# A wkv attention and expert-layer kernel on one core: VectorE's look at the chunk sums of w moves ahead of the output sum

## The chip, the core and the metric

The kernel runs on one NeuronCore of one Trainium2 chip. The metric is the device time of one execution in microseconds (us); a median of several runs is compared. TensorE is called PE in the profile, its weight loads PEld, VectorE DVE, ScalarE ACT, GpSimd POOL and SyncE SP.

## The reference, cut to what matters

```
for t in range(S):                                  # B=4, H=8, S=768, D=48
    y[:, :, t] = r_t @ (state + (u * k_t) v_t)      # per batch and head
    state = w_t[:, None] * state + k_t v_t
x = y as 3072 rows of 384
expert = argmax(x @ w_gate); gate = softmax(x @ w_gate)[expert]
out = gate * (relu(x @ w1[expert]) @ w2[expert])    # 8 experts, 384 -> 1024 -> 384
```

The first half is a linear attention with a decay w per position and channel; the second sends each of the 3072 rows to one of eight experts.

## The kernel before

**Tiling.** A half sequence of 384 positions is cut into 6 chunks of 64. Two heads share the 128 partitions (64 each, called sides), so a pass over one pair of heads and one half sequence is one iteration `i`, and there are NI = 32 of them: 4 batches, 4 pairs, 2 halves. Two iterations, an even one and the odd one after it, make a unit `un`. The attention fills the first half of the span, the experts the second. The order in which each engine gets its instructions is the order of the program text: nothing is reordered, and each engine works its own list through in that order, stopping at an instruction until the semaphores it needs are there.

**One iteration.** Iteration `i` prepares iteration `i + 2` and finishes `i - 2`. Its front, in the order of the text: ScalarE copies the chunk products of `i - 1` out of PSUM (`kv_out`, L605, out `PT`); TensorE transposes w of `i + 2` into bank `pw` (`tr_w`, L472) and the scaled keys of `i` into bank `pk` (`kb`, L550), ScalarE copies them out (`kb_out`, L557). VectorE adds the output of `i - 3` (`y_out`, L652: `py` plus `qv`, out `xr`), does a piece of routing if one is queued (`more`), and in even iterations scans the states of the last unit (`states`, L610: `PT` and `AT` in, `TT` out). Then it computes the decay of `i + 2`: a scan to `L` (L511), three small operations (L516, L517) and a scan to `F` (L524), both scans from bank `pw`. Behind that stands, in every fourth iteration, the look at w.

The body follows: GpSimd multiplies `qv` (L640) and `XB` (L537); TensorE transposes r (L480) and computes the scores (`sc`, L569); ScalarE copies the states to `RA` (L618) and `RB` (L621, even iterations; on VectorE, L623, for the last two units) and one side's scores to `XB` (L579); VectorE masks the other side's scores into `XA` (`sc_out`, L577). TensorE transposes k (L480), multiplies u (L488); ScalarE copies `kT` (L502) and `qs` (L494), and spreads w of `i + 3` into `gw` (`spread_w`, L446). VectorE multiplies `XA` (L535), `Kd` (L528) and `rk` (L441). TensorE ends its list for the iteration with the chunk sums of w (`w_sum(i + 2)`, L452), the chunk products (`kv(i)`, L597) and the output of `i - 2` (`y_mm`, L632), which reads `RA`, `RB`, `XA` and `XB`.

**The look at w.** `w_sum` writes 32 partitions of columns 144 to 271 of bank `pb` (`psP[1]`), a quarter for each of four iterations. `w_flag(g)` (L456) lets VectorE read all 128 x 128 of them once the four are there and puts the largest value of each partition into a column of `flags`; the flags decide at the end whether the slow path is needed. It runs in iterations 2, 6, 10, ..., 30, eight times. The same bank `pb` holds, in columns 0 to 143, half of what `kv` writes and `kv_out` reads. The four sums that `w_flag` in iteration 4g+2 reads were all issued by the end of iteration 4g+1, ahead of that iteration's `kv` and `y_mm`; the next sum, which overwrites a quarter, is issued near the end of iteration 4g+2.

```
def w_flag(g):
    nc.vector.tensor_scalar(wchk, psP[1][:, NB * D:NB * D + P], 0.0, None, op0=OP.max, op1=OP.max,
                            accum_out=flags[:, g:g + 1])
```

Of the kernel before, what the change touches and what calls it, by code (L numbers as in the profile page):

```python
# [38 lines left out]
def wkv_moe(ctx: ExitStack, tc: tile.TileContext, r, k, v, w, u, w_gate, w1, w2, out):  # L39
# [286 lines left out]
    def attention():  # L326
        NI = 2 * NP * B
        with ExitStack() as a:
# [67 lines left out]
            def more(n=1):  # L396
                for _ in range(min(n, len(todo))):
                    todo.pop(0)()

            def loads_wkr(b, h, g, hs=slice(0, HG)):  # L400
                if ("w", b, h, g) not in T:
                    T["w", b, h, g] = inp.tile([PW, HG, JW * D], F32, name="in_w", bufs=4)
                    T["rk", b, h, g] = inp.tile([P, 2, HG, 3 * D], F32, name="in_rk", bufs=4)
                ts = slice(h * HS, (h + 1) * HS)
                src = [x[b, g * HG:(g + 1) * HG, ts, :][hs] for x in (w, r, k)]
                nc.sync.dma_start(T["w", b, h, g][:, hs], src[0].rearrange("h (p j) d -> p h (j d)", j=JW))
                for n in range(2):
                    nc.sync.dma_start(T["rk", b, h, g][:, n, hs], src[1 + n].rearrange("h (p j) d -> p h (j d)", j=3))

            def loads_v(b, h, hs=slice(0, H)):  # L410
                if ("v", b, h) not in T:
                    T["v", b, h] = inp.tile([P, NB, H, D], F32, name="in_v")
                for q in range(NB):
                    t0 = h * HS + q * P
                    nc.sync.dma_start(T["v", b, h][:, q, hs], v[b, hs, t0:t0 + P, :].rearrange("h t d -> t h d"))
# [12 lines left out]
            def where(i):  # L428
                un, h = divmod(i, 2)
                b, pr = divmod(un, NP)  # L430
                return un, h, b, pr
# [23 lines left out]
# [3 lines that stand above are left out]
# [9 lines left out]
            def tr_w(i, psW=psW):  # L467
                T["pw", i] = psW[:GP]
                src = GW_[i % 2].rearrange("p j s x -> p j (s x)")
                pv = chunks(psW[:GP, :GW - 1], C + 1)[:, :, 1:].rearrange("p c (m j) -> p c m j", j=JW)  # L470
                for j in range(JW):
                    nc.tensor.transpose(pv[:, :, :, j], src[:, j, :GP], ident[:PW, :PW])  # L472
# [73 lines left out]
            def kb(i):  # L546
                p = bank("pk")
                Kf = KDM[i % 3].rearrange("p c x -> p (c x)")
                for q in range(NB):
                    nc.tensor.transpose(p[:, q * GP:(q + 1) * GP], Kf[:GP, q * P:(q + 1) * P], ident[:GP, :GP])  # L550
                nc.tensor.transpose(p[:, NB * GP:NB * GP + QR], T["qs", i], ident[:QR, :QR])
                T["pkb", i] = p

            def kb_out(i):
                n = NB * GP
                t = wk.tile([P, n + 32 * NB], F32, name="Kt")
                nc.scalar.activation(t[:, :n + QR], T["pkb", i][:, :n + QR], AF.Copy)  # L557
                T["Kt", i] = t[:, :n].rearrange("p (q x) -> p q x", x=GP)
                T["q", i] = t[:, n:].rearrange("p (q s) -> p q s", s=32)[:, :, :2]
# [27 lines left out]
            def npar(h, par):  # L587
                return NB - 1 if (h == 1 and par == 1) else NB
# [11 lines left out]
            def kv_out(i):  # L600
                un, h, b, pr = where(i)
                for par in range(2):
                    nq = npar(h, par)
                    c0 = h * NCH + par + 1
                    nc.scalar.activation(PT[un % 2][:GP, :, c0:c0 + 2 * nq - 1:2],  # L605
                                         psP[par][:GP, :nq * D].rearrange("p (q e) -> p e q", e=D), AF.Copy)
# [144 lines left out]
            def scatter(i, late):  # L751
                if 2 * i + late in SC:
                    more(len(todo))
                    for sb, q in SC[2 * i + late]:
                        route_s(rst[sb], q, scat)

            for i in range(NI):
                un, h, b, pr = where(i)
                rb = i % (2 * NP)
                nx = i + 2 < NI  # L760
                even = h == 0 and i > 0
                if b + 1 < B and rb in (0, 1, 4, 5):
                    loads_wkr(b + 1, rb % 4, rb // 4)
                if b + 1 < B and rb in (2, 7):
                    loads_v(b + 1, 0 if rb == 2 else 1)
                if ZF <= i < ZF + E:
                    e = i - ZF
                    zp = TOPB * TB // 4
                    nc.sync.dma_start(xs[e * NR:e * NR + TOPB * TB].rearrange("(q p) x -> p q x", p=zp),
                                      zrow[:zp, None, :].to_broadcast([zp, 4, ROW]))  # L770
                if b == B - 1 and rb == 3:
                    early_load()
                if b == B - 1 and 3 <= rb <= 6:
                    W[0][1](rb - 3)
                if i == 0:
                    for t in RA:
                        nc.gpsimd.memset(t[32:64], 0.0)
                    for t in RB:
                        nc.gpsimd.memset(t[96:128], 0.0)
                if i == 1:  # L780
                    nc.vector.memset(zrow, 0.0)
                    nc.vector.memset(zrow[:, DM + 1:].bitcast(U32), NT)
                if i > 0:
                    kv_out(i - 1)
                if nx:
                    tr_w(i + 2)
                kb(i)
                kb_out(i)
                final = i == NI - 1
                if final:  # L790
                    kv(i)
                    kv_out(i)
                if i >= 3:
                    y_out(i - 3)
                    more()
                if final:
                    states(un)
                scatter(i, 0)
                if even:
                    states(un - 1)  # L800
                    more()
                if nx:
                    decay(i + 2)
                if i % 4 == 2:
                    w_flag(i // 4)
                if i >= 1:
                    qv(i - 1)
                if nx:
                    tr(i + 2, "r")
                    r_out(i + 2)  # L810
                    r_mul(i + 2, 1)
                sc(i)
                if i >= NI - len(FILL[10]):
                    fill(FILL[10][i - NI])
                pe_route(i, 0)
                if even:
                    states_out(un - 1)
                sc_out(i, 1)
                sc_mask(i)
                sc_out(i, 0)  # L820
                if final:
                    states_out(un)
                more()
                pe_route(i, 1)
                if nx:
                    p = tr(i + 2, "k")
                elif i + 1 < NI:
                    p = bank("pt")
                if i + 1 < NI:
                    q_mm(i + 1, p)  # L830
                if nx:
                    k_out(i + 2)
                if i + 1 < NI:
                    q_out(i + 1)
                if i + 3 < NI:
                    spread(i + 3)
                    more()
                if nx:
                    r_mul(i + 2, 0)
                    more()  # L840
                    k_mul(i + 2)
                    more()
                    rk(i + 2)
                    a_out(i + 2)
                if i >= NI - len(FILL[0]):
                    fill(FILL[0][i - NI])
                if nx:
                    w_sum(i + 2)
                if not final:
                    kv(i)  # L850
                if i < 2:
                    warm(WARM[4 + i])
                if i >= NI - len(FILL[11]):
                    fill(FILL[11][i - NI])
                if i >= 2:
                    y_mm(i - 2)
                if h == 1 and un + 2 < NP * B:
                    loads_r(un + 2)
                scatter(i, 1)
                if rb == 1 and b == 3:  # L860
                    reserve("pk")
            i = NI
# [546 lines left out]
```

## Time and profile before

| what | us |
|---|---|
| median of 3 runs | 467.23 |
| lowest, highest | 464.39, 467.55 |
| the profiled execution: its own time | 468.12 |
| its span, first to last instruction | 466.4 |
| busy: PE, DVE, ACT, POOL | 413.2, 354.8, 282.1, 233.7 |

The rows further down are from the profiled execution. Each group of rows names its view. In the timeline a row gives the start in us from the start of the span, the duration in us, the engine, the line of the kernel, the operation, the tiles written and read, how many instructions are merged into the row, and in square brackets how long the engine sat idle before it and what it waited for. A releaser is inferred from semaphore events.

### The profile page before, as it was taken

The numbers are of one execution on the slowest core, as the hardware profiler recorded it, in microseconds if no ns is written. First come the engines' busy times: TensorE is split into PE (matmuls) and PEld (weight loads), VectorE is DVE, ScalarE is ACT, GpSimd is POOL, SyncE is SP. The second block draws the span as 40 slices with busy tenths as digits, with TensorE's granted clock in tenths as the row PEclk, the third lists the DMA queues.
The fourth block names the chain that finished last, engine by engine and source line by source line (L and its number), as shares of the span: only waits on it lengthen the run. The fifth ranks groups of instructions, "written<-read, shape, count | busy, mean of one in ns | idle before, by whom it ended". The sixth has DMA issues, their size and how long they took to land.

```text
span 466.4 us, 11637 instructions
## 1 busy us (share of the span) xinstructions
PE 413.2 (89%) x4427; PEld 367.0 (79%) x4427; DVE 354.8 (76%) x671; ACT 282.1 (60%) x536; POOL 233.7 (50%) x352
## 2 busy tenths in 40 slices
PE   6868798887889697888897999999999999999994
PEld 3556677666667586766787988999999999999994
DVE  7899898889999998877585788685857759585421
ACT  7758778887888878785363554544555445445210
POOL 6545344335665577433575010078484857758501
PEclk9879788897999988798999999999999999999999
DMA  7996669693784441560136989574565547450101
GB/s 194 227 221 154 152 163 296 182 248 98 178 217 105 104 93 52 158 207 25 52 126 153 285 187 214 154 198 128 164 142 183 155 156 207 145 173 31 51 20 33
DMA packets 120017, 70.32 MB, mean 151 GB/s; under 512 B 76231, under 2 KB 111268, under 8 KB 119951
## 3 DMA queue, kind: packets, MB, share of 16 engines
q1 hardware_dynamic: 115615, 60.01, 50.5%
q0 software_dynamic: 4336, 9.47, 5.8%
q8 instruction: 37, 0.61, 0.6%
q14 instruction: 29, 0.24, 0.2%
HBM read 54.07 MB, written 15.87 MB: 150 GB/s over the span
## 4 chain that ended last, share of the span: by engine, by line
PE 64%; DVE 14%; ACT 11%; DMA 4%; issue 4%; POOL 1%; POOLq 0%; DVEq 0%; ACTq 0%; SPq 0%
PE ps L1143 10%; PE pt L1143 5%; PE pw L1143 5%; PE ps L569 5%; PE pk L1130 5%; PE pk L1131 5%; PE pk L1129 5%; PE pt L480 3%; DMA wstage<-in_moe_w_dram 3%; DVE TT L610 3%; PE pw L472 3%; PE py L632 2%; PE py L1130 2%; PE py L1129 2%; PE py L1131 2%
## 5 line engine op out<-in xcount | busy, mean ns | idle before, releaser
L1199 POOL DMA_INDIRECT out_dram<-yo,yi x68 | 86.4, 1271 | 71.2 <-DVE yo L1195 55.7
L537 POOL TENSOR_TENSOR XB<-rT,F 64x384 f32<-64x384 f32 x32 | 31.5, 985 | 68.5 <-DVE F L524 36.1
L640 POOL TENSOR_TENSOR qv<-in_v,Kt 128x288 f32<-128x288 f32 x32 | 27.8, 868 | 26.6 <-DVE xr L652 19.5
L967 DVE TENSOR_TENSOR w2L<-wstage,w2H 128x1536 fp32r<-128x1536 f32 x16 | 33.0, 2060 | 7.6 <-ACT w2H L966 7.6
L480 PE MATMUL pt<-ident,grk 128*128 128x128 f32 x189 | 36.2, 306 | 1.5 <-ACT grk L461 0.8
L584 POOL TENSOR_SCALAR_AFFINE_SELECT XB<-XB 64x384 f32<-64x384 f32 x32 | 31.3, 979 | 7.9 <-ACT XB L579 6.2
L569 PEld LDWEIGHTS ps<-XA,Kd 64*64 64x64 f32 x384 | 29.5, 156 | 6.7 <-issue 5.2
L569 PE MATMUL ps<-XB,Kd 64*64 64x64 f32 x384 | 34.2, 246 | 0.0
L569 PE MATMUL ps<-XA,Kd 64*64 64x64 f32 x384 | 34.1, 246 | 0.0
L1143 PE MATMUL ps<-xH,w1H 128*128 128x256 f32 (+7 forms) x96 | 33.0, 344 | 1.2 <-DVE hL L1148 0.7
L967 DVE TENSOR_TENSOR w1L<-wstage,w1H 128x1536 fp32r<-128x1536 f32 x16 | 28.1, 1760 | 7.7 <-ACT w1H L966 7.6
L966 ACT ACTIVATE w2H<-wstage 128x1536 fp32r<-128x1536 f32 x16 | 31.6, 1981 | 2.4 <-DMA wstage<-in_moe_w_dram 2.4
L1143 PE MATMUL ps<-xH,w1L 128*128 128x256 f32 (+7 forms) x96 | 32.7, 342 | 0.0
L524 DVE TENSOR_TENSOR_SCAN F<-pw,bfw 128x390 f32<-128x390 f32 x31 | 30.1, 970 | 2.8
L511 DVE TENSOR_TENSOR_SCAN L<-pw,stepb 128x390 f32<-128x390 f32 x31 | 29.6, 955 | 2.7 <-PE pw L472 2.3
L266 POOL DMA_INDIRECT xs<-xr,slu x24 | 25.9, 1081 | 10.6 <-issue 4.6
L632 PE MATMUL py<-RB,XB 128*64 128x48 f32 x372 | 25.7, 234 | 5.8 <-issue 4.9
L1147 ACT ACTIVATE hH<-ps 128x256 fp32r<-128x256 f32 (+7 forms) x32 | 15.8, 493 | 24.4 <-PE ps L1143 24.4
L1143 PE MATMUL ps<-xL,w1H 128*128 128x256 f32 (+7 forms) x96 | 30.2, 341 | 0.0
L632 PE MATMUL py<-RA,XA 128*64 128x48 f32 x372 | 27.1, 239 | 2.7 <-ACT RA L618 2.0
L569 PEld LDWEIGHTS ps<-XB,Kd 64*64 64x64 f32 x384 | 29.4, 156 | 0.0
L1130 PE MATMUL pk<-hL,w2H 128*128 128x464 f32 (+4 forms) x80 | 28.4, 356 | 0.0
(284 smaller groups left out, 1367.7 us busy)
## 6 DMA issues: line engine op xcount, KB each, us to landing
wstage<-in_moe_w_dram SPq DMA_DIRECT2D x32, 768.0 KB
xs<-zrow SPq DMA_DIRECT2D x8, 723.8 KB
in_w<-in_w_dram SPq DMA_DIRECT2D x14, 288.0 KB
in_rk<-in_r_dram SPq DMA_DIRECT2D x14, 288.0 KB
in_rk<-in_k_dram SPq DMA_DIRECT2D x14, 288.0 KB
in_v<-in_v_dram SPq DMA_DIRECT2D x18, 192.0 KB
RA<-in_v_dram SPq DMA_DIRECT2D x16, 144.0 KB
RB<-in_v_dram SPq DMA_DIRECT2D x16, 144.0 KB
```

The costliest lines, as they stand in the source:

```text
L480: nc.tensor.transpose(pv[:GP, :, j], src[:, j, :GP], ident)
L537: nc.gpsimd.tensor_tensor(XB[un % 3][64:GP, h], rv[64:GP], F[64:GP], op=OP.mult)
L569: nc.tensor.matmul(T["psc", i, side][orow, c, :], KDM[i % 3][kr, c, :], X[un % 3][kr, h, c, :], start=True, stop=True)
L584: nc.gpsimd.affine_select(out=X[0:64, h], in_=X[0:64, h], compare_op=OP.is_gt, fill=0.0, base=0, pattern=[[0, NCH], [1, C]], channel_multi ...
L632: nc.tensor.matmul(p[64 * par:64 * par + 64, q, side, :], X[un % 3][:kr, h, c, :], R[un % 3][:kr, h * NCH + c, :], start=True, stop=True)
L966: nc.scalar.activation(hh, sv, AF.Copy)
L967: nc.vector.tensor_tensor(ll, sv, hh.bitcast(F32), op=OP.subtract)
L1129: nc.tensor.matmul(p, lh, rh, start=first, stop=False)
L1130: nc.tensor.matmul(p, lh, rl, start=False, stop=False)
L1131: nc.tensor.matmul(p, ll, rh, start=False, stop=last)
L1143: nc.tensor.matmul(p, ws["1" + x][:, c, sl], X[y, e][:, c, :n], start=(j == 0), stop=(j == len(terms) - 1))
L1199: d = nc.gpsimd.indirect_dma_start(out=out.rearrange("n (g x) -> (n g) x", g=XP), out_offset=bass.IndirectOffsetOnAxis(ap=X["i", e][:, q:q ...
```

## The change

The call of `w_flag` moves, within the same iteration, from behind the decay of `i + 2` to a place ahead of `y_out(i - 3)`. It keeps its condition, its data and its instruction. What it is moved past on VectorE's list: `y_out`, up to two queued routing operations, `states` in even iterations (all eight looks are in even iterations), and the operations of `decay(i + 2)` with a routing operation between them. Nothing is removed and nothing is added; no DMA is issued by it.

```
                 if final:
                     kv(i)
                     kv_out(i)
+                if i % 4 == 2:
+                    w_flag(i // 4)
                 if i >= 3:
                     y_out(i - 3)
                     more()
...
                 if nx:
                     decay(i + 2)
-                if i % 4 == 2:
-                    w_flag(i // 4)
                 if i >= 1:
                     qv(i - 1)
```

## Rows read from the trace of the kernel before

**Rows 1.** The page, its first line: span and instructions.
```profile
span 466.4 us, 11637 instructions
```

**Rows 2.** Waits of PE, attention stage: us in total, times, longest.
```profile
PE pb L452 <- DVE wchk L456: 17.0, 7, 3.5
PE pw L472 <- ACT gw L446: 7.9, 10, 1.1
PE pb L597 <- DVE wchk L456: 1.1, 1, 1.1
```

**Rows 3.** Waits of DVE, attention stage: same columns.
```profile
DVE TT L610 <- ACT PT L605: 4.6, 8, 1.5
```

**Rows 4.** Windows: stretch, its length, busy PE, PEld, DVE, ACT, POOL; clock.
```profile
24.00:226.00 202.00, 164.90 (x2913) 135.73 (x2912) 177.79 (x369) 157.90 (x346) 99.27 (x123) 0.87 0.59 153
```

**Rows 5.** The tile `wchk`: ns min/median/max, first and last start.
```profile
L456 DVE TENSOR_SCALAR_CACHE_REDUCE wchk<-pb x8: 265/266/278, 30.3 to 218.3; 128x128 bf16<-128x128 f32 x8
```

**Rows 6.** Timeline of DVE: `F` and the masked scores, iterations 14 and 16.
```profile
109.27 0.97 DVE L524 TENSOR_TENSOR_SCAN F<-pw,bfw 128x390 f32<-128x390 f32 x1
110.46 0.56 DVE L577 TENSOR_TENSOR XA<-ps,mask 64x384 f32<-64x384 f32 x1
...
123.39 0.97 DVE L524 TENSOR_TENSOR_SCAN F<-pw,bfw 128x390 f32<-128x390 f32 x1
124.39 0.56 DVE L577 TENSOR_TENSOR XA<-ps,mask 64x384 f32<-64x384 f32 x1
```

**Rows 7.** Timeline of ACT and PE, end of iteration 14.
```profile
109.11 1.21 ACT L621 ACTIVATE RB<-TT 48x576 f32<-48x576 f32 x1
110.48 0.59 PE L452 MATMUL pb<-gw,bones 96*32 96x128 bf16 x4 [2.61 <-DVE wchk L456]
111.38 0.52 ACT L446 ACTIVATE gw<-in_w 96x384 f32<-96x384 f32 x1
112.76 0.42 PE L632 MATMUL py<-RB,XB 128*64 128x48 f32 x4
113.11 0.90 PE L472 MATMUL pw<-ident,gw 96*128 96x96 f32 x4
```

**Rows 8.** Timeline of ACT and PE, end of iteration 16, without a look.
```profile
123.28 1.21 ACT L621 ACTIVATE RB<-TT 48x576 f32<-48x576 f32 x1
125.06 0.32 PE L632 MATMUL py<-RB,XB 128*64 128x48 f32 x4
126.13 0.55 PE L472 MATMUL pw<-ident,gw 96*128 96x96 f32 x4 [0.76 <-ACT gw L446]
```

**Rows 9.** Timeline of PE, iteration 30: first chunk product.
```profile
218.63 0.24 PE L597 MATMUL pb<-in_v,Kt 64*48 64x48 f32 x1 [1.14 <-DVE wchk L456]
```

**Rows 10.** Timeline of ACT and DVE, front of iteration 10.
```profile
78.78 0.46 DVE L652 TENSOR_TENSOR xr<-py,qv 128x288 f32<-128x288 f32 x1
79.50 0.24 ACT L605 ACTIVATE PT<-pb 128x96 f32<-128x96 f32 x1
79.78 1.48 DVE L610 TENSOR_TENSOR_SCAN TT<-PT,AT 128x576 f32<-128x576 f32 x1 [0.55 <-ACT PT L605]
```

**Rows 11.** Timeline of ACT and DVE, front of iteration 22.
```profile
158.54 0.23 ACT L605 ACTIVATE PT<-pb 128x96 f32<-128x96 f32 x1
158.81 0.45 DVE L652 TENSOR_TENSOR xr<-py,qv 128x288 f32<-128x288 f32 x1
```

**Rows 12.** Timeline of DVE: idle stretches behind iterations 2, 14 and 22.
```profile
33.43 0.46 DVE L652 TENSOR_TENSOR xr<-py,qv 128x288 f32<-128x288 f32 x1 [0.28 <-PE py L632]
34.18 0.97 DVE L511 TENSOR_TENSOR_SCAN L<-pw,stepb 128x390 f32<-128x390 f32 x1 [0.29 <-PE pw L472]
116.88 0.56 DVE L577 TENSOR_TENSOR XA<-ps,mask 64x384 f32<-64x384 f32 x1 [0.28 <-PE ps L569]
120.42 1.57 DVE L610 TENSOR_TENSOR_SCAN TT<-PT,AT 128x576 f32<-128x576 f32 x1 [0.41 <-ACT PT L605]
172.56 1.42 DVE L610 TENSOR_TENSOR_SCAN TT<-PT,AT 128x576 f32<-128x576 f32 x1 [0.19 <-ACT PT L605]
```

More of the change, by code (lines that the diff above doesn't have):

```diff
@@ L792, in attention @@
                     kv_out(i)
+                if i % 4 == 2:
+                    w_flag(i // 4)
                 if i >= 3:
@@ L803, in attention @@
                     decay(i + 2)
-                if i % 4 == 2:
-                    w_flag(i // 4)
                 if i >= 1:
```

## The prediction

> **What bounds the kernel now.** I read the span first [rows 1], then who waits for `wchk`, the tile that the moved instruction writes. There the largest wait of TensorE in the attention stage appears: the sum `w_sum` waited for VectorE's look seven times, 17.0 us together, and the first chunk product of iteration 30 once, 1.1 us [rows 2]. So the look isn't idle bookkeeping: TensorE, which runs ahead in iterations 2, 6, 10 and so on, stops at `w_sum(i + 2)` until VectorE has come through both scans to `w_flag`. The question is how much of these 18.1 us is on the path. The window over the stage answers half of it: of 202.0 us VectorE was busy 177.8, TensorE 164.9 [rows 4]. VectorE has only 24.2 us free in the whole stage and is what most iterations wait for in the end; a wait that goes away on TensorE is passed on only where VectorE in turn was waiting for TensorE.
>
> The rows at the end of iteration 14 against those of iteration 16, which has no look, give the other half. In iteration 14 the states reach `RB` at 109.11 + 1.21 = 110.32; `w_sum` starts at 110.48 and the output product ends at 112.76 + 0.42 = 113.18, which is 2.86 behind `RB` [rows 7]. In iteration 16 `RB` is there at 124.49 and the output product ends at 125.38, 0.89 behind it [rows 8]. So even with nothing to hold `w_sum` the output product waits for `RB`, and what the look costs TensorE is 2.86 - 0.89 = 1.97, not the 2.61 of the wait. What comes next, `tr_w` of the following iteration, needs `gw` from ScalarE, at 111.38 + 0.52 = 111.90 in iteration 14; it started at 113.11 [rows 7]. In iteration 16 it started 126.13 - 124.49 = 1.64 behind `RB`, released by `gw` [rows 8]. So the relief at `tr_w` is at most 113.11 - 111.90 = 1.21.
>
> **The change part by part.** *The instruction itself.* It lasts 0.27 us [rows 5], but instructions overlap on VectorE. Between the end of `F` and the masked scores lie 110.46 - 110.24 = 0.22 with the look and 124.39 - 124.36 = 0.03 without [rows 6]: it takes 0.19 of VectorE's list, 8 x 0.19 = 1.5 us in all. Nothing of this vanishes; it moves ahead of `y_out` and `TT`.
>
> *The wait removed.* `w_sum`, and with it `kv`, no longer waits. The relief at `tr_w`, measured as above to the end of `gw`, is 1.3 in iteration 2, 0.4 in 6, 1.2 in 14 and 1.25 in 22, and 0.06 in 10, 18 and 26, where ScalarE had a routing copy to make first and `gw` was the releaser anyway: 4.2 us at most. What is late next is `RB` and ScalarE's list up to `gw`.
>
> *The wait added.* At the front of the iteration the look needs the sums, which were issued ahead of the previous iteration's products, so they are no obstacle. But the look reads bank `pb`, and ScalarE reads other columns of `pb` (`PT`) just there: in iteration 10 from 79.50 to 79.74, while `y_out` ran from 78.78 to 79.24 [rows 10]. If the two reads are kept apart, the look waits for `PT`, and behind it on VectorE stand `y_out`, the routing piece, `TT`, `L` and `F`; ScalarE's `RA` and `RB` wait for `TT`, GpSimd's next `qv` for `y_out`. No row shows two engines' reads of one bank in a fixed order. The nearest row is the one of iteration 30, where a product written to columns 0 to 143 waited 1.14 us for a look at columns 144 to 271 [rows 9]: the order is kept by bank, not by column. From below the wait costs nothing (no order among reads), from above it costs until the end of `PT` plus look plus `y_out`. I take the upper end, since the row of iteration 30 is nearest to it.
>
> What the added wait makes of `TT`: in iteration 10 the look starts at 79.76, takes 0.22, `y_out` follows at 79.98 and `TT` about 0.4 later, at 80.38 in place of 79.78; `TT` took 1.48 instead of 1.35 there since it began at the very end of `PT`, so its end is 0.47 later [rows 10]. In iteration 22 `PT` was done at 158.77 when `y_out` began at 158.81 [rows 11]: no wait, only the look's own 0.2. Read in the same way the eight are 0.2 in 2, 22 and 30, about 0.3 in 6, and 0.35 to 0.5 in 10, 14, 18 and 26: 2.6 us together. In 26 a ScalarE copy stands ahead of `RA` and hides it.
>
> The Trainium skill (PSUM — Partial Sum Buffer, section PSUM bank collisions raise a hardware error) says that two engines must not be in one bank and the same partitions at once, reads against reads included and whatever the columns. By it the added wait is real and the sum is the one below; without it the sum would be 0.7 lower, the third rival. No run here shows it for two reads.
>
> *The sum.* Iteration 2: VectorE waited 0.28 for `py` and 0.29 for `pw` right behind it [rows 12]; `tr_w` comes 1.1 earlier net of the 0.2, so about 0.5 of this is gained. Iteration 6: 0.4 of relief against 0.3 of delay, 0.1 gained. Iteration 14: `tr_w` net 0.8 earlier; VectorE's next waits on that chain are 0.28 and 0.41 [rows 12], against 0.17 lost on `F`: 0.5 gained. Iteration 22: only 0.19 of waiting behind it [rows 12], 0.2 gained. Iteration 30: the product waits no more, the output product is then held by `RA`, 0.2 later than now: 0.2 gained. Iterations 10 and 18: no relief, `RA` and `RB` later by 0.3 and 0.4, lost. Iteration 26: 0. Together 0.5 + 0.1 + 0.5 + 0.2 + 0.2 - 0.3 - 0.4 = 0.8 us gained. The expert stage behind it starts from the last rows of the attention and only shifts. The profiled execution took 468.12 (span 466.4 and 1.7 around it), so 467.3 by its own clock; the median of the runs is 0.9 below that execution, so **466.4**.
>
> **The rivals.** *Slower, the front of the even iteration decides.* All looks fall in even iterations, whose `TT`, `RA`, `RB` feed the output product; if VectorE takes none of the relief, the delays of `TT` stay: 2.6 less the 0.38 of iteration 26, 2.2, so 469.4. For it: `TT` waits for `PT` 4.6 us in all already [rows 3], so the front is tight, and VectorE is 88% busy [rows 4]. Against it: the waits behind iterations 2 and 14 [rows 12]. It decides as soon as fewer than two of these waits close. *Relief carried on whole.* If the relief at `tr_w` stays on the path, 4.2 less 1.1 of delay in the four iterations with relief and less the 0.7 of iterations 10 and 18 leaves 2.4 to 3.1: about 464.3. For it: TensorE's clock was 0.87 in the stage, and in iteration 14 the last products are slower than in 16 (0.42 against 0.32 for four [rows 7, 8]), and a shorter idle time may keep the clock up. Against: VectorE's 24.2 free us are spread over 202. *No added wait.* The look slides into the idle time ahead of `TT` (0.55 in iteration 10 [rows 10]); then 6 and 18 are 0.1 and 0.2 better, and so on: 1.5 gained, 465.7. *The whole wait on the path.* The output product's delay against iterations without a look, 1.97 in iteration 14 and 9 over the eight, 458. Only if `gw` came much earlier than it does.
>
> **Chances.** Forecast 0.43; slower at the front 0.22; relief whole 0.13; no added wait 0.13; whole wait 0.04; something not seen here 0.05. About 1%, some 4.7 us, is what a measurement of this kernel can tell from no change; the runs shown spread over 3.2 us. All but the last two cases lie within it: same 0.89, faster 0.07 (the whole wait, and a part of the relief case), slower 0.04. The range goes from 463.5 (relief whole, with a part of the runs' spread) to 469.3 (all delays, no relief).
>
> **What would show it.** In the profile after: no wait of `pb` on `wchk`; the look starting right behind `PT<-pb` where that was late (iterations 6, 10, 18) and right behind `rk` in 22; the masked scores 0.03 behind `F` in all even iterations; the output product of iteration 14 ending about 0.9 behind `RB`; `TT` later against its `PT` by 0.4 to 0.6 in iteration 10. It is wrong if `y_out` runs ahead of the look, if the look starts before `PT<-pb` ends, or if `tr_w` in iterations 3, 15 and 23 is still more than 1.7 behind `RB`.

## The result, and the profile after

Twenty executions of each kernel, taken together, gave a median of 465.35 us after the change against 466.57 us before. The comparison that is quoted for them is a ratio of 0.9893 with a 95% interval of 0.9851 to 0.9934. It is made over the runs within 1.5% of each kernel's own fastest, and since the changed kernel scatters more (457.6 to 472.9 us, one run at 566.84 apart, against 460.5 to 472.8), this bound lies lower for it and the ratio shows more than the whole does. Over all executions collected in the study for which the granted clock is listed, 38 after (without the one at 566.84) and 81 before, the means are 464.7 and 466.8 us: a ratio of 0.9955, interval 0.9921 to 0.9989 by resampling the runs. The change saves about 2 us (2.1, with a standard error of 0.8). The predicted 466.4, a gain of 0.8, has the right sign but less than half of that size; I took the change for one that cannot be told from none, and the gain has another reason than the one I gave.

The table has these executions, the mean granted TensorE clock of the whole span (1 is full speed), and the time at equal clock; ± is one standard error. For the last column one line was fitted through all kernels with a common slope (3.24 us less for each 0.01 of clock, uncertain by 0.13) and one offset for each kernel, the offsets given against the kernel before. The column is a reading of scatter, not an experiment: it splits each difference into a part that goes with the clock and a rest. For the filled kernels at the end, whose clock lies far off, the offset leans on the slope and says little.

| kernel | runs | mean us | clock | at equal clock, us |
|---|---|---|---|---|
| before | 81 | 466.8 ± 0.3 | 0.9435 ± 0.0007 | 0 |
| after | 38 | 464.7 ± 0.8 | 0.9519 ± 0.0022 | +0.6 ± 0.3 |
| look behind TT | 24 | 464.1 ± 0.7 | 0.9470 ± 0.0020 | -1.6 ± 0.4 |
| no look | 6 | 464.8 ± 1.8 | 0.9492 ± 0.0051 | -0.1 ± 0.7 |
| look in front, sums held | 6 | 471.2 ± 1.3 | 0.9348 ± 0.0035 | +1.6 ± 0.7 |
| before, look's pauses filled | 12 | 463.1 ± 0.3 | 0.9612 ± 0.0011 | +2.0 ± 0.5 |
| before, other pauses filled | 12 | 463.0 ± 0.7 | 0.9567 ± 0.0020 | +0.5 ± 0.5 |
| before, all 14 filled | 6 | 458.3 ± 0.9 | 0.9828 ± 0.0019 | |
| after, all 14 filled | 6 | 458.1 ± 0.7 | 0.9820 ± 0.0015 | |
| behind TT, all 14 filled | 6 | 457.8 ± 0.9 | 0.9805 ± 0.0026 | |

The clock of the changed kernel is higher on each of the two chips on which both kernels have runs with a clock: 0.956 against 0.945 and 0.950 against 0.944.

**The waits went as forecast.** The profiled execution of the changed kernel took 467.31 us, span 465.5, which is above its median; it is read for what waits for what, not for the gain. Its last output sum of the attention starts at 230.56 us, against 230.63 in the profile before, so nearly all of the 0.9 us by which its span is shorter lies behind the attention. First TensorE's waits in the stage from 24 to 226 us, the view of [rows 2]:

```profile
PE pw L472 <- ACT gw L446: 12.3, 14, 1.1
PE py L632 <- issue: 9.5, 11, 1.0
PE py L632 <- ACT RA L618: 7.6, 10, 1.7
```

Neither wait on `wchk` is left. But the idle time was not saved: the window over the stage, the view of [rows 4], says that TensorE was busy as long (164.88 us, 164.90 before), and so idle as long.

```profile
24.00:226.00 202.00, 164.88 (x2911) 134.07 (x2910) 175.44 (x369) 157.74 (x346) 101.95 (x123) 0.88 0.60 153
```

The waits on `gw` rose from 7.9 to 12.3 us, those of the output product on `RA` and on what the profile does not name to 7.6 and 9.5. In the same view of the kernel before they were:

```profile
PE py L632 <- issue: 4.9, 6, 1.0
PE py L632 <- ACT RA L618: 2.0, 4, 0.6
```

The timeline of iteration 14, ScalarE and TensorE, answers to [rows 7]:

```profile
108.31 0.39 PE L452 MATMUL pb<-gw,bones 96*32 96x128 bf16 x4
110.08 1.21 ACT L621 ACTIVATE RB<-TT 48x576 f32<-48x576 f32 x1
110.11 0.32 PE L632 MATMUL py<-RA,XA 128*64 128x48 f32 x4 [0.99 <-ACT RA L618]
111.39 0.32 PE L632 MATMUL py<-RB,XB 128*64 128x48 f32 x4 [0.96 <-issue]
111.86 0.32 PE L632 MATMUL py<-RB,XB 128*64 128x48 f32 x4
112.36 0.52 ACT L446 ACTIVATE gw<-in_w 96x384 f32<-96x384 f32 x1
112.94 0.55 PE L472 MATMUL pw<-ident,gw 96*128 96x96 f32 x4 [0.76 <-ACT gw L446]
```

The sums no longer wait, the output product ends 112.18 - 111.29 = 0.89 behind `RB` (2.86 before), and `tr_w` starts 1.65 behind it (2.79 before), released by `gw`. The pause of 2.61 us is cut into pieces of 0.99, 0.96 and 0.76 us with work between them.

**The added wait is there too.** The timeline of VectorE and ScalarE at the front of iteration 6, and of iteration 10, which answers to [rows 10]:

```profile
53.57 0.23 ACT L605 ACTIVATE PT<-pb 128x96 f32<-128x96 f32 x1
53.84 0.29 DVE L456 TENSOR_SCALAR_CACHE_REDUCE wchk<-pb 128x128 bf16<-128x128 f32 x1 [1.03 <-ACT PT L605]
54.05 0.45 DVE L652 TENSOR_TENSOR xr<-py,qv 128x288 f32<-128x288 f32 x1
54.42 1.35 DVE L610 TENSOR_TENSOR_SCAN TT<-PT,AT 128x576 f32<-128x576 f32 x1
...
79.70 0.23 ACT L605 ACTIVATE PT<-pb 128x96 f32<-128x96 f32 x1
80.01 0.29 DVE L456 TENSOR_SCALAR_CACHE_REDUCE wchk<-pb 128x128 bf16<-128x128 f32 x1
...
80.60 1.35 DVE L610 TENSOR_TENSOR_SCAN TT<-PT,AT 128x576 f32<-128x576 f32 x1
```

In iteration 6 VectorE sat idle for 1.03 us ahead of the look, until ScalarE's read of the same bank was done, with the output sum queued behind it; `TT` starts 0.62 behind the end of `PT` (53.80), where it started 0.02 behind it in the trace before. In iteration 18 the same wait is 1.01. In iteration 10 there was no wait of this kind: `rk`, just ahead on VectorE's list, ended at 79.98, later than `PT` (79.93), and `TT` starts 0.67 behind `PT` (0.04 before) because the look and the output sum now stand between them.

**Where the clock differs.** Over the whole stage this pair of profiles has nearly the same clock, 0.87 and 0.88. Windows over the stretch behind iteration 14's pause, where the kernel before ran at half clock throughout, before and after (the last number but two is the granted clock):

```profile
110.00:116.70 6.70, 6.22 (x87) 5.50 (x86) 6.20 (x19) 4.54 (x12) 3.14 (x3) 0.50 0.15 28
```

```profile
110.00:116.70 6.70, 4.87 (x64) 4.16 (x64) 6.42 (x19) 5.66 (x14) 3.14 (x3) 0.77 0.02 3
```

0.50 is the lower of the two levels (1.2 of 2.4 GHz) all through; with the pause in pieces it is 0.77. In windows of 1 us the half clock lasts from about 109.9 to 116.7 before, and after the change from about 113.6 to 117.0: it comes later and is half as long, but it comes. One stretch proves little, since the clock falls at other places in other executions; the case for the clock rests on the runs below.

### The profile page after: what moved, and what is told of

It is laid out like the page before. It is cut to its first block, busy times and chain, and to the rows that moved or that the text cites. A ratio compares the mean times of both kernels' runs of the same rounds, so it can differ in the third digit from the quotient of the medians.

```text
span 465.5 us, 11642 instructions
## 1 busy us (share of the span) xinstructions
PE 412.8 (89%) x4425; PEld 365.9 (79%) x4427; DVE 352.5 (76%) x671; ACT 282.0 (61%) x536; POOL 238.6 (51%) x352
## 4 chain that ended last, share of the span: by engine, by line
PE 61%; DVE 15%; ACT 12%; issue 5%; DMA 3%; POOL 2%; SPq 0%; POOLq 0%; ACTq 0%; DVEq 0%
PE ps L1143 11%; PE pw L1143 6%; PE pt L1143 6%; PE pk L1130 5%; PE pk L1131 5%; PE pk L1129 5%; PE ps L569 4%; DVE TT L610 3%; PE pt L480 3%; PE py L1130 3%; PE py L1129 3%; PE py L1131 3%; PE pw L472 2%; ACT RB L621 2%; ACT gw L446 2%
## 5 line engine op out<-in xcount | busy, mean ns | idle before, releaser
L640 POOL TENSOR_TENSOR qv<-in_v,Kt 128x288 f32<-128x288 f32 x32 | 26.8, 838 | 25.7 <-DVE xr L652 18.7
L480 PE MATMUL pt<-ident,grk 128*128 128x128 f32 x189 | 37.2, 312 | 1.4 <-ACT rT L498 0.8
L584 POOL TENSOR_SCALAR_AFFINE_SELECT XB<-XB 64x384 f32<-64x384 f32 x32 | 33.2, 1039 | 7.5 <-ACT XB L579 5.8
L632 PE MATMUL py<-RB,XB 128*64 128x48 f32 x372 | 24.5, 227 | 12.4 <-issue 9.5
L266 POOL DMA_INDIRECT xs<-xr,slu x24 | 27.7, 1153 | 9.4 <-issue 3.2
L632 PEld LDWEIGHTS py<-RB,XB 128*64 128x64 f32 x372 | 20.6, 141 | 13.8 <-issue 10.6
L472 PE MATMUL pw<-ident,gw 96*128 96x96 f32 x124 | 19.3, 286 | 13.4 <-ACT gw L446 12.3
```

What stands on the lines that cost most here:

```text
L480: nc.tensor.transpose(pv[:GP, :, j], src[:, j, :GP], ident)
L584: nc.gpsimd.affine_select(out=X[0:64, h], in_=X[0:64, h], compare_op=OP.is_gt, fill=0.0, base=0, pattern=[[0, NCH], [1, C]], channel_multi ...
L632: nc.tensor.matmul(p[64 * par:64 * par + 64, q, side, :], X[un % 3][:kr, h, c, :], R[un % 3][:kr, h * NCH + c, :], start=True, stop=True)
```

## The experiments

Three theories were set against each other: the path alone (1), TensorE's clock (2), and a gain in the expert stage (3). The first four ran on one chip with the kernel before.

**The changed kernel again.** No edit.

> The changed kernel once more, for a second execution of it beside the kernel before. The first comparison gave 465.35 against 466.57 in the medians of 20 runs each, single runs from 457.6 to 472.9, and the profiled execution reached the last output sum of the attention at 230.56 in place of 230.63. Theory 1 (the path: a little relief, a little delay): a median 0 to 2 us under the kernel before, the last output sum of the attention within 1.5 us of 230.6. Theory 2 (TensorE's clock: the pause ahead of the chunk sums is shorter, and the granted clock in the attention stage is higher in more of the executions): in an execution under 461 us the stage from 24 to 226 us shows a clock of 0.92 or more against 0.87 before, and the gain lies in the attention, 4 us or more. Theory 3 (the gain lies behind the attention, in the expert stage): an execution under 461 us has its last output sum at 230 us all the same.

Measured: 463.8 mean of 7, clock 0.956, times from 457.4 at a clock of 0.974 to 474.1 at 0.933. The profiled one (474.08) reached its last output sum at 234.49 us with a clock of 0.88 over the stage; the first profile of this kernel had 230.56. So two executions of one program differ by 3.9 us at the end of the attention, more than theory 1 has to give. The stage's clock was 0.88 in both, so this pair does not show that the clock makes the difference; this execution lies 3.3 us above the line of time against clock, about which the executions scatter by 1.5 us (standard deviation). No profile of an execution under 461 us was had, so theory 3 is not excluded for these by a profile of the changed kernel itself; it is for the filled kernels below, whose attention ends earlier as their clock is higher. From the start of the last output sum to the end of the span the fourteen profiles of this study need 234.7 to 237.6 us, in no order of kernel or clock (234.9, 237.6 and 234.8 for the changed kernel, 235.8 and 236.9 for the kernel before).

**The look behind TT.**

```
                 if even:
                     states(un - 1)
+                if i % 4 == 2:
+                    w_flag(i // 4)
+                if even:
                     more()
                 if nx:
                     decay(i + 2)
-                if i % 4 == 2:
-                    w_flag(i // 4)
```

> The look stands behind the scan of the states and ahead of the decay, so that the output sum and the scan do not wait for it, while TensorE's chunk sums still find it done before L and F. Theory 1: the delay of TT of 0.2 to 0.5 us in each of eight fronts is gone and the relief stays: TensorE's wait on wchk under 3 us in all (18.1 before), VectorE's wait on PT as before (TT 4.6 us), the attention about 2 us earlier than in the kernel before. Theory 2: the pause is as short as in the changed kernel, so the times scatter as there and the median is equal within 2 us.

Measured: 465.2 mean of 12, clock 0.944, and at equal clock below both kernels. TensorE's waits on the look in its profile:

```profile
PE pb L452 <- DVE wchk L456: 1.4, 2, 1.2
```

The relief is there without the delay, and it is worth something on the path: 1.6 us at equal clock, and 2.2 between this place and the front. That difference is what I had put on the delays of `TT` (2.2 us). One more wait, of a chunk product, is 0.6 us. The profile's last output sum came 2.9 us before that of the kernel before, but single profiles scatter by as much, and its stage clock was 0.90. The wait of `TT` on `PT` was 3.2 us there, not the 4.6 that I had expected to see again.

**No look at all.** The two lines are taken out.

> The look at w is left out altogether (the eight columns of flags keep their first value), so neither the 0.19 us of VectorE nor a wait on either side remains. Theory 1: no wait on wchk, 1.5 us of VectorE's list saved, no delay of TT: the attention 2.5 to 3.5 us earlier than in the kernel before. Theory 2: about the same time as the changed kernel, within 2 us, with a clock of 0.88 or more from 24 to 226 us. The difference of this kernel to the changed one is the price of the wait that the change added.

Measured: 464.8 mean of 6, clock 0.949. Its profile (464.16 us) had no wait on `wchk`, a stage clock of 0.92 and the last output sum at 227.59, 3.0 us earlier, as theory 1 wanted; yet over the six runs nothing is gained at equal clock (-0.1 ± 0.7). The profile alone would have confirmed theory 1 by the luck of its clock. Why the look's absence should be worth less than its place behind `TT` isn't settled; six runs are few.

**The look in front, the sums held as before.**

```
                 if nx:
                     decay(i + 2)
+                if i % 4 == 2:
+                    nc.vector.memset(psP[1][:, 500:501], 0.0)
                 if i >= 1:
                     qv(i - 1)
```

on top of the changed kernel.

> The changed kernel with one more small VectorE write, to an unused column of the bank pb, at the place where the look stood before: the look stays in front, but TensorE's chunk sums are held until VectorE has come through F, as before the change. Theory 1: TensorE waits some 17 us again and the delay of TT comes on top: 1 to 2.5 us slower than the kernel before. Theory 2: the pause ahead of the chunk sums is back, so the clock from 24 to 226 us is 0.87 or less and the time that of the kernel before or up to 2.5 us more. If it is as fast as the changed kernel, the wait of TensorE is not what the change bought.

Measured: 471.2 mean of 6 and ratio 1.012 [1.007, 1.017], clock 0.935. TensorE's waits in its profile:

```profile
PE pb L452 <- DVE pb L807: 18.9, 7, 3.6
```

It is 6.5 us slower than the changed kernel, from which it differs by one write of one column in eight iterations. At equal clock only 1.0 ± 0.7 of these are left; the rest goes with the clock, 0.935 against 0.952. So with the look in front it is the release of the chunk sums that the changed kernel's clock comes from. Two things do not fit as neatly. The kernel is also 4.4 us slower than the kernel before, more than the 2.5 I had allowed, at a clock lower by 0.009, though the sums are held about as long in both (18.9 and 17.0 us): the release is not all that sets the clock, or six runs are too few. And its profiled execution, the quickest of the six (465.72 us), had a stage clock of 0.90, above the 0.87 that theory 2 wanted; the means carry the argument, not that profile.

**The kernel before against itself.**

> The kernel before once more, unchanged, against itself: what one comparison says when nothing differs, and how far two executions of one kernel lie apart in the trace. All theories: a ratio whose interval holds 1, a mean within 2 us of 466.5, a mean granted clock of 0.945 within 0.005, and single executions that lie on the same line as the others (about 3.3 us less for each 0.01 of mean clock).

Measured: ratio 1.0006 [0.9964, 1.0049], 467.2 mean of 12, clock 0.944, as expected. Its profile reached the last output sum at 228.64 with a stage clock of 0.90, 2.0 us earlier than the first profile of the same program (230.63 and 0.87).

**Idle matmuls in the pauses.** On the kernel before, and the same two lines on the changed kernel and on the one with the look behind `TT`:

```
+                if nx and even:
+                    warm(6)
                 if nx:
                     w_sum(i + 2)
```

> The kernel before with six idle matmuls (ones times ones into bank py, which the output product overwrites) ahead of the chunk sums in the 14 even iterations 2 to 28. The look stays where it was, so TensorE's chunk sums are held as before; only the pause ahead of them is filled with 1.3 us of work at full clock. Theory 2 (the change pays through the granted clock, since the clock falls where TensorE pauses in even iterations): the mean clock rises by 0.01 or more over 0.945 and the time falls by 3 us or more, though no wait was taken off any chain; at equal clock the time is that of the kernel before or up to 1 us more. Theory 1 (the path alone): the same time or up to 2 us more, since the filling takes nothing off and lies ahead of the output product.

Measured: 458.3 mean of 6, ratio 0.9814 [0.9753, 0.9876], clock 0.983. The look is where it was, the sums are held, and VectorE's list is the same; 84 matmuls that nobody reads make the kernel 8.5 us faster. The window over the stage and TensorE's wait on the look:

```profile
24.00:226.00 202.00, 176.66 (x3080) 135.47 (x3095) 184.91 (x385) 159.82 (x356) 110.14 (x134) 0.97 0.61 157
```

```profile
PE pb L452 <- DVE wchk L456: 8.4, 6, 2.2
```

A clock of 0.97 where [rows 4] had 0.87. The last output sum is at 222.05 in place of 230.63: VectorE comes through the same list 8.6 us earlier. Up to the end of that output sum it was busy 200.5 us and idle 30.6 in the kernel before, busy 203.1 and idle 19.4 here; its wait for ScalarE's copy `kT` of a TensorE product alone fell from 7.4 to 2.1 us. So what I had read as VectorE's bound had waiting in it that a quicker TensorE shortens. By the common line this kernel lies 4.2 us above the kernel before at equal clock, where I had expected 0 to 1: whether that is the price of the idle matmuls, or the line is not straight so far out, isn't known.

> The changed kernel with the same six idle matmuls in the 14 even iterations. Theory 2: the clock rises over that of the changed kernel (0.952) as well, and the time falls by 2 us or more below it; if the filling makes the clock of this kernel and of the filled kernel before alike, their times differ by less than 2 us, since at equal clock the changed kernel has shown no advantage. Theory 1: as the changed kernel or up to 2 us more.

Measured: 458.1 mean of 6, ratio 0.983 [0.9771, 0.9889], clock 0.982.

> The look straight behind the scan of the states (where it delays neither the output sum nor TT, and TensorE's wait on wchk is nearly gone) with the six idle matmuls. At equal clock that place has been about 2 us better than before and after, but its clock was that of the kernel before (0.944). Theories 1 and 2 together: both gains add up, a clock of 0.955 or more and a mean of 461 us or less, the fastest of the kernels. If the clock does not rise, it stays at 464 to 466.

Measured: 457.8 mean of 6, ratio 0.9809 [0.9744, 0.9875], clock 0.981. The clock rose as expected, but the mean is that of the other two within its error, and not visibly lower: with the clock near full the place of the look no longer shows. The three filled kernels agree within 0.5 us, each uncertain by about 0.8: with the clock held up, the change is worth 0.2 ± 1.1 us. All three beat both kernels of the case by more than 6 us.

**Which pauses.** The filling only in the seven iterations with a look, and only in the seven without:

```
+                if nx and i % 4 == 2:
+                    warm(6)
```

```
+                if nx and even and i % 4 == 0:
+                    warm(6)
```

> The kernel before with the six idle matmuls only in the 7 iterations that have a look and a preparation (2, 6, ..., 26): the pause that the change takes away is filled, and nothing else. Theory 2: these pauses cost the clock what the change gives back or more, so the mean clock rises from 0.943 to 0.953 or above and the time falls by 3 to 6 us; filling all 14 gave a clock of 0.983 and 8.7 us. If the clock stays under 0.948, the pauses at the look are not what the changed kernel's clock comes from.

> The kernel before with the six idle matmuls only in the 7 even iterations without a look (4, 8, ..., 28), which the change does not touch: the other half of the filling. Theory 2: it raises the clock too, by 0.015 to 0.03, since the clock fell behind these iterations as well (at 69, 96, 120 and 175 us in the profile before); together with the filling of the look's pauses the two rises add up to about the 0.04 of all 14.

Measured: filling the look's pauses raised the clock by 0.018 and took 3.7 us off; the others 0.013 (a little less than expected) and 3.8 us. I had listed the clock as falling behind iteration 12 too (at 96 us); read again, the profile before shows 1.00 there, and half clock behind 4, 8, 16, 24 and 28. The windows over the stage, first the one with the look's pauses filled:

```profile
24.00:226.00 202.00, 171.94 (x3013) 136.35 (x3011) 181.68 (x376) 156.94 (x346) 102.05 (x126) 0.92 0.60 153
```

```profile
24.00:226.00 202.00, 170.51 (x3020) 134.91 (x3018) 181.52 (x378) 157.73 (x351) 106.28 (x128) 0.93 0.60 155
```

The two rises add up to 0.031 of the 0.039 that both together give. The pauses at the look thus cost about half of the clock that the filled pauses cost in all, and the change, which cuts them up without filling them, gets back 0.008 of it.

**Both contenders once more.**

> The changed kernel a third time, for a profile of one of its quicker executions and a surer mean of the clock: 26 runs gave 464.3 us and a clock of 0.9527, against 467.0 and 0.9432 for the kernel before. Theory 2: a mean clock of 0.949 to 0.957, the times on the line of about 3.4 us less for each 0.01 of clock, within 1.5 us of the kernel before at equal clock; an execution with a clock of 0.96 or more has its last output sum of the attention at 226 us or earlier (230.6 in the two profiles with 0.94).

> The look straight behind the scan of the states, a second time: 12 runs gave a clock of 0.9444 and a time 1.4 us under the kernel before at equal clock. Theory 1: again 1 to 2 us under the kernel before at equal clock, since TT is not delayed. Theory 2 in its simple form (TensorE's pause at the look alone sets the clock) wants a clock of 0.950 or more here, as the wait on wchk is as good as gone; a clock of 0.945 again says that the pause at the look is not the whole of it.

Measured: the changed kernel 465.5 mean of 12 at a clock of 0.950, the look behind `TT` 463.0 at 0.9495, both beside 466.5 at 0.944. The profile of the changed kernel was again of an execution above the median (469.29, last output sum at 232.65 with a stage clock of 0.86), so the expectation on one with a clock of 0.96 stays untested. For the place behind `TT` this set alone lies 1.8 us under the kernel before at equal clock, as theory 1 expected; the mean clock over both sets, 0.947 ± 0.002, lies between the kernel before and the limit of 0.950 that I had set: whether its clock is that of the changed kernel is not settled.

## Why the prediction was wrong

**The mechanics were mostly right.** The wait of 18.1 us on the look is gone; the look waits for ScalarE's read of the same bank in iterations 6 and 18 (not in 10, where `rk` was later), and `y_out` and `TT` behind it; the output product of iteration 14 ends 0.9 behind `RB`; `tr_w` of iterations 3, 15 and 23 starts 1.64 to 1.65 behind `RB`, released by `gw`. The masked scores of iteration 14 start at 111.25, 0.03 behind the end of `F`:

```profile
110.25 0.97 DVE L524 TENSOR_TENSOR_SCAN F<-pw,bfw 128x390 f32<-128x390 f32 x1
111.25 0.56 DVE L577 TENSOR_TENSOR XA<-ps,mask 64x384 f32<-64x384 f32 x1
```

**The path term was a little off.** I summed 0.8 us gained; at equal clock the changed kernel is 0.6 ± 0.3 us slower. The delay was sized well (2.2 ± 0.4 us between the place in front and the place behind `TT`), the relief probably too high: the look behind `TT`, which has the relief with next to no delay, gains 1.6 ± 0.4 us at equal clock, where the sum of 0.8 with its 2.2 of delay added back whole would have 3.0. That the kernel without a look, which has no delay either, gains nothing at equal clock (-0.1 ± 0.7) leaves the size of the relief open.

**The step that failed is the sum itself, which has no term for the clock.** I held that a wait taken off TensorE counts only where VectorE in turn waited for TensorE, and used a clock row only as a point in favour of one rival, relief carried on whole. The premise under it, that VectorE has only its 24.2 free us to give and is the bound, fell with it: with all 14 pauses filled VectorE was idle for 19.4 us in place of 30.6 up to the last output sum. The granted clock was in the trace ([rows 4]: 0.87 over the stage; the slower products of [rows 7] against [rows 8]), and its price could have been asked for: at 0.87 a quarter of the stage ran at half clock. The fitted line puts the term at 0.0084 more clock times 324 us, 2.7 us gained (with a standard error of 0.8), less 0.6 on the path: the 2.1 measured; the two parts are a split by the line, not two measurements. That the clock is worth time is shown by filling those same pauses without releasing anything (0.961, 3.7 us faster), and that the changed kernel's clock hangs on the release by holding the sums again (0.935, 6.5 us slower). That the cut-up pause rather than the total of idle time is what spares the clock is argued from one stretch (0.50 to 0.77 behind iteration 14) and from the equal idle total; it was not tested by itself, and the place behind `TT`, whose pauses are cut up in the same way, has not clearly shown it.

**The rivals.** *Slower, the front decides* was right in its sign at equal clock and in what the front place costs against the place behind `TT` (2.2 us), but the net is 0.6 ± 0.3 slower, not 2.2, and the clock outweighs it. *Relief carried on whole* named the clock and gave 464.3, close to the pooled 464.7, yet by the wrong sum, since the relief is not carried on. *No added wait* fell by the row of iteration 6, and *the whole wait on the path*, 458, by the means after the change: 464.7, and at equal clock no gain. The sentence from the Trainium skill on reads of one bank (PSUM — Partial Sum Buffer, PSUM bank collisions raise a hardware error) agrees with the trace after the change: 1.03 and 1.01 us of waiting by a read for another engine's read of other columns. That the program orders them is what the trace shows; what would happen without the order no run tried.

**The range** of 463.5 to 469.3 holds both the median of 465.35 and the pooled mean. That rests partly on luck: the clock's share and the path's error have opposite signs.

## What to carry to other kernels

Where the granted clock of a stage lies well under 1, put a term for it into the sum: ask what each pause of TensorE does to the stretch behind it, not only whether its end is on the path. Taking a long wait off TensorE can pay through the clock though no chain gets shorter, and filling this kernel's pauses with matmuls that nobody reads paid four times as much (8.5 us against 2.1) and left no difference between the places of the look that six runs each could show. Judge such kernels by many executions with their clock beside the time: a single profile here would have confirmed a wrong theory.

## What the runs showed of the hardware that I had not expected

The time of one program varies by 3.6% (457.4 to 474.1 us for the changed kernel) along one line with the mean granted clock, 3.24 us less for each 0.01 more, and the correlation is -0.94 over 38 runs. In the profile before, the stretches at half clock from 110.0 to 116.7 (0.50) and from 164.5 to 168.0 (0.52) follow the pauses of iterations 14 and 22; after the change the first shows 0.77, but the second 0.54 all the same, so in these two executions a pause in pieces went with more clock in one place and not in the other. And six idle matmuls of 0.38 us in the trace, ahead of work that was waiting anyway, cost less than the clock gave back: with 84 of them the kernel before ran 8.5 us faster.
